# Another order of the parts of an attention step, and one more copy of the transposed keys on VectorE

## The chip, the cores and the metric

The kernel runs on one core of a Trainium2 chip. Its time is device microseconds (us) of one execution. Engines are named as the profile names them: PE is TensorE's matmul, PEld its weight loads, DVE is VectorE, ACT is ScalarE, POOL is GpSimd, SP is SyncE, which issues the DMAs. Each engine works through its own queue in order.

## The reference

Three parts follow each other; everything is float32.

```python
# attention, q, k, v: (4, 8, 576, 64)
out_d = sm_attn(q_d, k_d, v_d)          # on means of 4 tokens
out_up = np.repeat(out_d, factor, axis=2)
mask = np.abs(pos[:, None] - pos[None, :]) < factor
...
out_local = np.matmul(attn, v)          # softmax over the band of 7 tokens
x = out_up + out_local                  # -> (2304, 512)
# soft mixture of experts, 8 experts with 4 slots each
logits = x @ phi
slot_input = softmax(logits, axis=0).T @ x
h = np.maximum(slot_input[e] @ w1[e], 0.0); slot_out[e] = h @ w2[e]
y = softmax(logits, axis=1) @ slot_out
# feed-forward
h = np.maximum(y @ w_in, 0.0)
out = h * h @ w_out
```

## The kernel before

The attention works on 16 units; a unit is one batch and a pair of heads, four units make a batch. It is a software pipeline written out by hand: step s of 19 runs a string of letters, each letter is one part, and the part is that of unit s minus the letter's lag (table LAG). All steps use the string ORDER, except those in the table ORDERS (0 to 3 and 15 to 18 before). The order of the letters is the order of the instructions in each engine's queue; two parts that use different engines don't see each other's place in the string.

The parts that matter here, with their engines:

- Q, L (SP): load q and k, or v, of a unit; l and o (SP): load the next LOADN or LOADO expert weights into a ring of 32 buffers.
- T, K (PE, then ACT and DVE): transpose q, or k, of a unit into two PSUM tiles `tr`, one for each head (line 412), and copy each by two copies, of 64x320 and 64x256, into `qt` (line 423) or `kz` (line 419). The tuple DCOPY names the (is k, head, half) whose copy DVE makes; ACT makes the others. One `qt` and one `kz` buffer serve all units.
- M, S (PE): the band mask and the local scores into the bank `s` (lines 443, 454). R (DVE): their maximum and its subtraction (465, 466); E (ACT): exp (471); n (DVE): sums and reciprocal (501, 502); P (POOL): probabilities `pl` (508); p (PE, DVE): their transposes and copies `pt` (527, 528).
- d, b (POOL): sums of four tokens of q and of k (436, 438). s (PE): scores of those (479); m (DVE): maxima (486, 487); e (ACT): exps `pd` (493); N (DVE, POOL): normalisation `sm` and `pn` (515 to 517); q (PE, ACT, DVE): transposes `pdp` and copies `pdt` (556, 557).
- V, v, w, D, A: values (570), their sums and transposes (537, 545, 547), the downsampled values and their scaled copy `xd` on ACT (583, 588), and the addition `xt` on DVE (596).
- t, X, Y: logits of a unit (612), token rows (631, 639). With the last unit of a batch, t also issues the batch softmax `mb`, `nm`, `ee`, `eb` on DVE and ACT (655 to 668), and g and G its transposes and the sum `sip` and `acc` (676 to 700).
- F, H, J (PE): so many filler matmuls of 128x256 in bf16 (line 364), whose result nobody reads; table FN gives the number for each step. START is the number of fillers ahead of step 0. c: a step of narrowing the feed-forward weights, if they are there (CONV).

Below, "S of unit 9" is the part S, and "the letter q" the part q. After step 18 comes a chain that closes the batch softmax (lines 812 to 838, ending with `sT`), then eight experts (888 to 917), then the feed-forward (1044 to 1138).

Of the kernel before, what the change touches and what calls it, by code (L numbers as in the profile page):

```python
# [18 lines left out]
B, H, S, D = 4, 8, 576, 64  # L19
# [16 lines left out]

MAG_LO = 2.0 ** -15
MAG_HI = 1.875 * 2.0 ** 16 - 2.0 ** -7
CONV = {10: 1, 12: 1, 15: 3, 18: 1, 19: 2}
TCH = 384  # L40
LOOK = 2
W32 = 5
LBE = 5
LOADN = {0: 1, 1: 2, 2: 2, 3: 2, 4: 1, 5: 3, 6: 4, 7: 3, 8: 3, 9: 2, 10: 2, 11: 4, 12: 3, 13: 4, 14: 4, 15: 2, 16: 4, 17: 3, 18: 4, 19: 4}
LOADO = {0: 1, 1: 1, 2: 1, 3: 0, 4: 2, 5: 0, 6: 1, 7: 0, 8: 0, 9: 0, 10: 2, 11: 0, 12: 2, 13: 0, 14: 0, 15: 3, 16: 1, 17: 4, 18: 3, 19: 4}
ORDER = 'YFSgREVLvqwndGKHJsmDPeTAoptQMbNXcl'
LAG = {'Q': -2, 'L': 0, 'T': 0, 'K': 0, 'd': 1, 'b': 0, 'M': 0, 'S': 1, 'R': 1, 's': 1, 'E': 1, 'm': 1, 'n': 1, 'P': 1, 'e': 1, 'N': 1, 'v': 2, 'q': 2, 'p': 1, 'w': 2, 'V': 2, 'D': 2, 'A': 2, 't': 2, 'X': 2, 'Y': 3, 'g': 3, 'G': 3}
LASTS = 3
ORDERS = {0: 'YAsFvSgKToGdpDlHqJRPcEVewnMNXtQbmL', 1: 'YSgREVFvqdJwnGKLsmDAPeToHlptQbMcNX', 2: 'YFcVSgRLEvqJwnKdsmPDAeToptQbHlGMNX', 3: 'YgSREVLFvqJwnKdsmDAeToHPGplctQbMNX', 15: 'YJSgREVFLvqwndKsmDAeToPHGpctQbMlNX', 16: 'YFSgREVLvqJdwnKlsmGDAeToPHpctQbMNX', 17: 'YJEFSgRVLvqwnPTKdsMDAmeoGHlctQbNXp', 18: 'YEVFLvqJSgDeRwnKdsmAToGHPlptQbcMNX'}
FN = {'F': [0, 1, 1, 0, 0, 0, 0, 0, 0, 0, 0, 0, 0, 0, 0, 4, 0, 10, 0, 0], 'H': [10, 5, 2, 0, 0, 0, 0, 0, 0, 0, 0, 0, 0, 0, 0, 1, 0, 4, 0, 0], 'J': [1, 4, 3, 0, 0, 0, 0, 0, 0, 0, 0, 0, 0, 0, 0, 0, 7, 3, 0, 0]}  # L50
LATE = 16
LOADS = 'Q0 L0 phi Q1 L1'
START = 24
DDVE = ()
DCOPY = ((1, 0, 1),)
PCOPY = (0, 5, 4)
CHAIN = (2, 4, 4)
NEG = -6.25e7
# [23 lines left out]
def attention_moe_ffn_kernel(  # L82
# [105 lines left out]
    def load_next(n=1):  # L188
        for _ in range(n):
            if not loads or not free:  # L190
                return
            kind, i, j = loads[0]

            fits = [x for x in free if x[0] is not wa or kind in ("w1", "w2") and i == 0 and int(x[1][1:]) >= WRES]
            fits.sort(key=lambda x: x[0] is not wa)
            if kind == "wout" or kind == "win" and (j > 0 or LPOS[i] > 50 or lb is None) or kind != "win" and i == NE - 1:
                fits = [x for x in free if x[0] is ring]
            elif kind != "win" and i >= LBE + 1:
                fits = [x for x in fits if x[1][0] != "b"]
                fits.sort(key=lambda x: x[0] is ring)  # L200

            if kind == "wout" or kind == "win" and j > 0:
                if sum(x[0] is ring for x in free) <= 2 + parts[0]:
                    return
            if not fits:
                return
            place = fits[0]
            free.remove(place)
            loads.popleft()
            load(kind, i, j, place)  # L210
# [87 lines left out]
    def narrow_next(n=1):  # L298
        for _ in range(n):
            narrow_turn()  # L300
# [10 lines left out]
    with tc.tile_pool(name="att", bufs=1, side="right") as ap:  # L311
# [49 lines left out]
        def busy(n, start=False):  # L361

            for _ in range(n):
                nc.tensor.matmul(warm, warmb, warmw, start=start, stop=True, skip_group_check=True)  # L364
# [38 lines left out]
        def transposes(u, js=(0, 1)):  # L403
            st = U[u]
            for j in js:
# [7 lines left out]
                for h, t in enumerate(ts):  # L413
                    hr = slice(64 * h, 64 * h + 64)
                    to = (kzs[u % QKB][hr, h] if j else qs[u % QKB][hr])[:, 3:3 + S].rearrange("p (c r) -> p c r", r=9)
                    for r in range(2):
                        o, i_ = to[:, :, r:9:2], t[64 * r:64 * r + 64, 0:5 - r].rearrange("p i c -> p c i")
                        if j:
                            (nc.vector.tensor_copy if (j, h, r) in DCOPY else nc.scalar.copy)(out=o, in_=i_)  # L419
                        elif (j, h, r) in DCOPY:  # L420
                            nc.vector.tensor_scalar(out=o, in0=i_, scalar1=1.0 / 128.0, scalar2=None, op0=ALU.mult)
# [346 lines left out]
        def run(x, s):  # L768
# [6 lines left out]
            elif x in "lo":  # L775
                load_next((LOADN if x == "l" else LOADO).get(s, 1))
            elif x in FN:
                busy(FN[x][s])
            elif x == "c":
                narrow_next(CONV.get(s, 0))  # L780

# [5 lines left out]
        tm.enter_context(tc.manual_schedule())  # L787
        busy(START, True)
        for s in range(NU + LASTS):
            for x in ORDERS.get(s, ORDER) + ("a" if s == LATE else ""):  # L790
                if x == "a":
# [405 lines left out]
```

## Time and profile before

| | us |
|---|---|
| median of 3 runs | 432.02 (431.2 to 434.45) |
| the profiled execution | 431.98 |
| its span, first to last instruction | 430.3 |
| mean granted TensorE clock in the span | 0.992 |

Between the profiled execution and its span lie 1.7 us outside all instructions. The attention fills the first 153 us, the closing chain ends with `sT` at 161.7 us, the experts run to 197 us and the feed-forward to the end. A row of the timeline gives start, duration, engine, line and operation; several instructions of one kind are merged with their count, and their duration is then from the first start to the last end. In brackets stands the idle time of the engine before the row, with what released it.

### The profile page before, as it was taken

What the parts mean: (1) busy time and instruction counts of PE and PEld (TensorE: products, weight loads), DVE (VectorE), ACT (ScalarE), POOL (GpSimd) and SP (SyncE); (2) the same over time, 40 slices, a digit from 0 to 9 for tenths busy, and PEclk for the clock granted to TensorE, in tenths of its full rate; (3) what the DMA queues carried; (4) which work ended last, traced back from release to release, by engine and by line L of the source; (5) the groups of instructions that cost most, each with busy time, mean ns of one, the idle gap of its engine ahead of it and who ended that gap; (6) DMA issues with size and microseconds to landing.
All of it is one profiled execution on the core that took longest, in us unless ns stands there. A gap on an engine that the chain in (4) does not pass through costs nothing.

```text
span 430.3 us, 11647 instructions
## 1 busy us (share of the span) xinstructions
PE 402.4 (94%) x4534; PEld 308.2 (72%) x4534; DVE 300.7 (70%) x713; ACT 270.6 (63%) x670; POOL 116.2 (27%) x225
## 2 busy tenths in 40 slices
PE   7798899899998989997999999999999999999994
PEld 5566667657766755554877888888888888888883
DVE  3566666666666542396999897897899777665663
ACT  4578768767867422245897587777875655545640
POOL 7576556655656300130000600005000320000000
PEclk9999999999999989999999999999999999999998
DMA  6998999999831489999990001020000000012232
GB/s 178 366 254 259 291 293 340 274 282 288 208 96 33 149 249 368 411 407 407 408 390 8 0 0 50 1 100 0 2 0 0 2 1 2 0 74 75 75 133 87
DMA packets 43249, 70.55 MB, mean 164 GB/s; under 512 B 24378, under 2 KB 24634, under 8 KB 43194
## 3 DMA queue, kind: packets, MB, share of 16 engines
q1 hardware_dynamic: 43050, 69.68, 49.1%
q8 instruction: 36, 0.59, 0.6%
q14 instruction: 19, 0.16, 0.1%
q10 hardware_dynamic: 144, 0.13, 0.1%
HBM read 65.07 MB, written 4.72 MB: 162 GB/s over the span
## 4 chain that ended last, share of the span: by engine, by line
PE 59%; DVE 3%; ACT 1%; issue 1%; DVEq 0%; ACTq 0%
PE po L1125 44%; PE up L1044 4%; PE so L917 4%; PE hp L888 3%; PE ap L1002 1%; DVE glo L1057 0%; DVE part L1107 0%; PE lgt L364 0%; DVE r L1053 0%; PE warm L930 0%; PE ctp L722 0%; DVE win L234 0%; DVE win L233 0%; PE arp L1015 0%; PE crp L867 0%
## 5 line engine op out<-in xcount | busy, mean ns | idle before, releaser
L1125 PE MATMUL po<-wparts,ghi 128*128 128x512 f32 x576 | 148.8, 392 | 0.2 <-DVE part L1107 0.2
L1125 PEld LDWEIGHTS po<-wparts,ghi 128*128 128x128 f32 x576 | 106.8, 188 | 20.5 <-DVE part L1107 0.6
L1125 PE MATMUL po<-wparts,glo 128*128 128x512 f32 x288 | 81.7, 391 | 0.5 <-DVE glo L1057 0.5
L1049 ACT ACTIVATE r<-up 128x384 f32<-128x384 f32 x96 | 47.0, 490 | 55.5 <-PE up L1044 48.2
L1057 DVE TENSOR_TENSOR glo<-r,ghi 128x384 fp32r<-128x384 f32 x94 | 52.2, 558 | 22.0 <-ACT ghi L1056 18.6
L1125 PEld LDWEIGHTS po<-wparts,glo 128*128 128x128 f32 x288 | 54.0, 188 | 13.3 <-DVE glo L1057 0.9
L1029 POOL COPY selq<-asb 32x128 f32<-32x128 f32 x48 | 20.3, 422 | 138.0 <-ACT asb L1010 135.4
L1053 DVE TENSOR_TENSOR r<-r 128x384 f32<-128x384 f32 x48 | 26.8, 559 | 17.4 <-ACT ghi L1052 17.4
L1044 PE MATMUL up<-cst,ast 128*128 128x384 f32 x96 | 33.0, 344 | 1.1 <-ACT cst L874 1.1
L508 POOL TENSOR_TENSOR pl<-elp,sm 64x350 f32<-64x350 f32 x32 | 24.6, 770 | 31.9 <-PE tr L412 21.9
L419 ACT COPY kz<-tr 64x320 f32<-64x320 f32 (+1 forms) x48 | 20.5, 428 | 15.1 <-PE tr L412 14.3
L423 ACT ACTIVATE qt<-tr 64x320 f32<-64x320 f32 x64 | 28.0, 437 | 1.2
L1052 ACT ACTIVATE ghi<-r 128x384 fp32r<-128x384 f32 x50 | 26.3, 526 | 1.6
L1055 ACT ACTIVATE r<-r 128x384 f32<-128x384 f32 x46 | 24.2, 526 | 1.5
L465 DVE TENSOR_REDUCE mx<-s 128x10 f32<-128x350 f32 x16 | 8.3, 517 | 23.3 <-PE s L454 23.3
L1056 ACT CAST ghi<-r 128x384 fp32r<-128x384 f32 x46 | 23.6, 514 | 1.4
L436 POOL TENSOR_TENSOR s<-kz 64x288 f32<-64x288 f32 x32 | 21.2, 661 | 5.9 <-DVE kz L419 3.8
L1109 DVE TENSOR_TENSOR part<-po,part 128x512 f32<-128x512 f32 x36 | 22.6, 683 | 0.0
L1044 PEld LDWEIGHTS up<-cst,ast 128*128 128x128 f32 x96 | 18.0, 188 | 5.9 <-ACT cst L874 1.6
L471 ACT ACTIVATE elp<-elp 128x350 f32<-128x350 f32 x16 | 7.9, 496 | 20.8 <-DVE elp L466 20.8
L454 PE MATMUL s<-kz,qt 128*29 128x70 f32 x640 | 13.0, 225 | 7.5 <-ACT qt L423 7.5
L517 POOL TENSOR_TENSOR pn<-pd,sm 128x435 f32<-128x435 f32 x16 | 14.6, 914 | 15.5 <-DVE sm L516 7.9
(209 smaller groups left out, 715.0 us busy)
## 6 DMA issues: line engine op xcount, KB each, us to landing
w<-in_moe_w_dram SPq DMA_DIRECT2D x64, 512.0 KB, 7.6
win<-in_moe_w_in_dram SPq DMA_DIRECT2D x16, 512.0 KB, 10.2
wout<-in_moe_w_out_dram SPq DMA_DIRECT2D x16, 512.0 KB, 10.2
vw<-in_v_dram SPq DMA_DIRECT2D x62, 80.0 KB, 6.0
q<-in_q_dram SPq DMA_DIRECT2D x16, 288.0 KB, 5.7
k<-in_k_dram SPq DMA_DIRECT2D x16, 288.0 KB, 5.9
out_dram<-o SPq DMA_DIRECT2D x17, 256.0 KB, 2.1
vw<-in_v_dram SPq DMA_DIRECT2D x2, 64.0 KB, 2.7
```

What stands on the lines that cost most here:

```text
L423: nc.scalar.mul(out=o, in_=i_, mul=1.0 / 128.0)
L436: nc.gpsimd.tensor_tensor(out=s1[r], in0=t[:, :, 0], in1=t[:, :, 1], op=ALU.add)
L508: nc.gpsimd.tensor_tensor(out=pl[r, :, c0:c0 + W], in0=el[r], in1=sm[r, 0:NB].unsqueeze(2).to_broadcast([64, NB, W]), op=ALU.mult,)
L1044: nc.tensor.matmul(t, ast[:, 128 * f:128 * f + 128], cst[:, c * n:c * n + n], start=True, stop=True)
L1049: nc.scalar.activation(out=r, in_=t, func=AF.Relu)
L1052: nc.scalar.activation(out=ghi, in_=r, func=AF.Square)
L1053: nc.vector.tensor_tensor(out=g, in0=r, in1=r, op=ALU.mult)
L1055: nc.scalar.activation(out=g, in_=r, func=AF.Square)
L1056: nc.scalar.copy(out=ghi, in_=g)
L1057: nc.vector.tensor_tensor(out=glo, in0=g, in1=ghi, op=ALU.subtract)
L1109: nc.vector.tensor_tensor(out=part[c, i], in0=po[c][i], in1=part[c, i], op=ALU.add)
L1125: nc.tensor.matmul(po[c][i], a[:, 128 * i:128 * i + 128], w[f], start=(first and w is whi and a is ghi), stop=(last and a is glo), skip_gr ...
```

## The change

It changes tables only. DCOPY gets a second entry: the 64x320 copy of the first head's transposed k, made by ACT before, is made by DVE in every unit. (These are transposed keys of the attention; the copies of slot probabilities further down are as they were.) ORDER and ORDERS put the letters in another order; step 3 now uses ORDER. START falls from 24 to 12 and FN gives the fillers to other steps. LOADN, LOADO and CONV are changed at some steps.

```diff
-CONV = {10: 1, 12: 1, 15: 3, 18: 1, 19: 2}
+CONV = {5: 1, 7: 1, 10: 2, 11: 1, 14: 1, 15: 2, 19: 3}
...
-ORDER = 'YFSgREVLvqwndGKHJsmDPeTAoptQMbNXcl'
+ORDER = 'clYSRgVdEvqHJwFnLGKsmoDAeTPpbNQtXM'
...
-FN = {'F': [0, 1, 1, 0, 0, 0, 0, 0, 0, 0, 0, 0, 0, 0, 0, 4, 0, 10, 0, 0], 'H': [10, 5, 2, 0, 0, 0, 0, 0, 0, 0, 0, 0, 0, 0, 0, 1, 0, 4, 0, 0], 'J': [1, 4, 3, 0, 0, 0, 0, 0, 0, 0, 0, 0, 0, 0, 0, 0, 7, 3, 0, 0]}
+FN = {'F': [0, 1, 5, 0, 0, 0, 0, 0, 0, 0, 0, 0, 0, 0, 0, 3, 0, 9, 0, 0], 'H': [8, 6, 1, 0, 0, 0, 0, 0, 0, 0, 0, 0, 0, 0, 0, 3, 6, 7, 1, 0], 'J': [2, 7, 5, 0, 0, 0, 0, 0, 0, 0, 0, 0, 0, 0, 0, 0, 5, 2, 0, 0]}
...
-START = 24
+START = 12
 DDVE = ()
-DCOPY = ((1, 0, 1),)
+DCOPY = ((1, 0, 1), (1, 0, 0))
```

Seen by engine: POOL's queue is the same, row for row. ACT's loses the 16 copies of 64x320 and is otherwise the same from the second step on. DVE's gains them, no narrowing moves to another place in it, and the two small operations of N stand in another place in three steps. On PE, M and X change places in the steps, and the fillers are elsewhere (83 before the chain, 80 in the old kernel). On SP the same loads stand in another order among each other.

**DVE, the step that ends the second batch** (`sm` is N's, `mb` to `lst` the batch softmax, `acc` the letter G's, `kz` the letter K's, `mx<-sdb` the letter m's). Before:

```order
L528 COPY pt<-sdb 128x2x58
L655 TENSOR_REDUCE mb_1799<-lgt 128x1
...
L645 COPY lst<-lgt 128x16
L515 TENSOR_SCALAR sm_1671<-sm_1671 128x3
L516 RECIPROCAL sm_1671<-sm_1671 128x3
L465 TENSOR_REDUCE mx_1863<-s_1817 128x10
...
L698 SCALAR_TENSOR_TENSOR acc<-acc,al_1801,sip_1918 128x512
```

Now:

```order
L528 COPY pt<-sdb 128x2x58
L515 TENSOR_SCALAR sm_1675<-sm_1675 128x3
L516 RECIPROCAL sm_1675<-sm_1675 128x3
L655 TENSOR_REDUCE mb_1818<-lgt 128x1
...
L645 COPY lst<-lgt 128x16
L465 TENSOR_REDUCE mx_1866<-s_1838 128x10
...
L698 SCALAR_TENSOR_TENSOR acc<-acc,al_1820,sip_1926 128x512
L419 COPY kz_146<-tr_10_1933 64x64x5
L419 COPY kz_146<-tr_10_1933 64x64x4
L486 TENSOR_REDUCE mx_1866<-sdb 128x2
```

N's two operations moved ahead of the batch softmax; the copy of 64x64x5 is new, between `acc` and the old copy. In the steps that end no batch, that copy is the only difference.

**PE, the first units** (`tr_1*` is k's transpose, `tr_0*` q's; 175 and 177 are unit 0's, 187 unit 1's k). Before:

```order
L364 MATMUL lgt<-warmb 128x256
L412 MATMUL tr_10_219<-ident,k_177 128x64
...
L412 MATMUL tr_01_236<-ident,q_175 64x64
L364 LDWEIGHTS warmb
...
L454 MATMUL s_266<-kz_146,qt_143 29x70
...
L412 MATMUL tr_11_312<-ident,k_187 64x64
L479 MATMUL sdb<-qkd 64x144 x2
```

Now:

```order
L412 MATMUL tr_01_208<-ident,q_175 64x64
L364 LDWEIGHTS warmb
...
L412 MATMUL tr_10_231<-ident,k_177 128x64
...
L454 MATMUL s_261<-kz_146,qt_143 29x70
...
L412 MATMUL tr_11_293<-ident,k_187 64x64
L364 LDWEIGHTS warmb
...
L479 MATMUL sdb<-qkd 64x144 x2
```

Before, 24 fillers, k, q, 11 fillers, M, S of unit 0, 5 fillers, k of unit 1 and directly the letter s. Now 12 fillers, q, 8 fillers, k, 2 fillers, M, 1 filler, S, k of unit 1, then 13 fillers ahead of the letter s. In the next step 5 fillers stand between w and k of unit 2, where 3 stood ahead of w.

**PE, the last units** (`av<-pdt,vd` is D of unit 14, `ptp` and `sdb<-ident,pl` the letter p of unit 15, the last, `av<-pt,vw` its V). Before:

```order
L583 MATMUL av_0_2932<-pdt_2957,vd_2981 64x48 x4
L527 MATMUL ptp_0_3010<-ident,pl 128x128 x4
L527 MATMUL sdb<-ident,pl 128x128
...
L639 MATMUL av_1_2933<-ident,xt_3002 64x128
L364 LDWEIGHTS warmb
...
L570 MATMUL av_0_3058<-pt,vw_140 64x73
```

Now:

```order
L583 MATMUL av_0_2929<-pdt_2954,vd_2968 64x48 x4
L364 LDWEIGHTS warmb
...
L527 MATMUL ptp_0_3011<-ident,pl 128x128 x4
L527 MATMUL sdb<-ident,pl 128x128
...
L639 MATMUL av_1_2930<-ident,xt_2999 64x128
L364 LDWEIGHTS warmb
...
L570 MATMUL av_0_3055<-pt,vw_140 64x73
```

Six fillers stand ahead of p, where none stood; ahead of V it is 9 fillers, 13 before. Between D of unit 15 and the letter t of that unit it is 9, 4 before.

## Rows read from the trace of the kernel before

**Rows 1.** The page's head: span, and busy time of each engine.

```profile
span 430.3 us, 11647 instructions
PE 402.4 (94%) x4534; PEld 308.2 (72%) x4534; DVE 300.7 (70%) x713; ACT 270.6 (63%) x670; POOL 116.2 (27%) x225
```

**Rows 2.** Timeline of PE in a regular step: start, duration, operation, [idle before].

```profile
96.76 0.82 PE L454 MATMUL s<-kz,qt 128*29 128x70 f32 x40 [0.52 <-ACT qt L423]
...
99.50 0.67 PE L412 MATMUL tr<-ident,k 64*128 64x64 f32 x10
...
100.73 0.77 PE L583 MATMUL av<-pdt,vd 75*64 75x96 f32 x16
...
104.85 0.37 PE L454 MATMUL s<-kz,qt 128*29 128x70 f32 x10 [0.53 <-ACT qt L423]
```

**Rows 3.** Timeline of ACT in the same step.

```profile
100.21 1.34 ACT L419 COPY kz<-tr 64x320 f32<-64x320 f32 x3 [0.18 <-PE tr L412]
101.60 0.41 ACT L588 ACTIVATE xd<-av 128x288 f32<-128x288 f32 x1
101.91 0.37 ACT L493 ACTIVATE pd<-sdb,mx 128x144 f32<-128x144 f32 x1
...
102.97 1.82 ACT L423 ACTIVATE qt<-tr 64x320 f32<-64x320 f32 x4
```

**Rows 4.** Timeline of DVE in the same step.

```profile
100.69 0.43 DVE L419 COPY kz<-tr 64x256 f32<-64x256 f32 x1 [0.56 <-ACT kz L419]
```

**Rows 5.** Waits of 0 to 140 us: engine and line, releaser, total, times, longest.

```profile
PEld av L583 <- ACT kz L419: 2.0, 10, 0.2
```

**Rows 6.** Groups of 0 to 140 us by form: busy us, mean ns of one, idle before.

```profile
L528 DVE COPY pt<-ptp 128x464 f32<-128x464 f32 x15 | 9.5, 634 | 1.3 <-PE ptp L527 1.3
...
L419 DVE COPY kz<-tr 64x256 f32<-64x256 f32 x16 | 6.9, 431 | 9.2 <-ACT kz L419 8.9
```

**Rows 7.** Timeline of the step that ends the second batch.

```profile
87.24 1.21 PE L570 MATMUL av<-pt,vw 64*64 64x73 f32 x40
...
87.55 0.92 POOL L517 TENSOR_TENSOR pn<-pd,sm 128x435 f32<-128x435 f32 x1 [2.50 <-ACT xr L640]
...
91.82 0.75 DVE L698 SCALAR_TENSOR_TENSOR acc<-acc,al,sip 128x512 f32<-128x512 f32 x1 [1.61 <-PE sip L695]
...
92.64 0.43 DVE L419 COPY kz<-tr 64x256 f32<-64x256 f32 x1
```

**Rows 8.** Timeline of the first units.

```profile
1.15 5.30 PE L364 MATMUL lgt<-warmb 128*128 128x256 bf16 x24 [1.15 <-DVE warmb L315]
...
12.30 0.34 PE L479 MATMUL sdb<-qkd 64*64 64x144 f32 x2
...
14.25 0.46 DVE L486 TENSOR_REDUCE mx<-sdb 128x2 f32<-128x288 f32 x1
...
17.76 0.82 PE L454 MATMUL s<-kz,qt 128*29 128x70 f32 x40
...
20.80 0.52 PE L412 MATMUL tr<-ident,k 64*128 64x64 f32 x10 [0.22 <-ACT pdt L557]
```

**Rows 9.** The load of unit 1's k: issue, and us from issue to landing.

```profile
L376 SPq DMA_DIRECT2D k<-in_k_dram x1: 430/430/430, 6.0 to 6.0; - x1
...
DMA to landing us min/median/max: 4.2/4.2/4.2
```

**Rows 10.** Timeline of PE in the last two steps.

```profile
147.33 1.58 PE L364 MATMUL lgt<-warmb 128*128 128x256 bf16 x13
...
151.95 0.61 PE L364 MATMUL lgt<-warmb 128*128 128x256 bf16 x4
...
153.44 0.54 PE L612 MATMUL lgt<-xt,phis 128*32 128x128 f32 x16 [0.88 <-DVE xt L596]
```

**Rows 11.** Stretches around 154 us: length, busy of each engine, PEclk, DMA share, GB/s.

```profile
152.00:153.50 1.50, 0.62 (x10) 0.32 (x12) 0.83 (x2) 0.41 (x1) 0.00 (x0) 1.00 0.91 232
...
154.50:155.50 1.00, 1.00 (x7) 0.64 (x6) 0.37 (x4) 0.70 (x3) 0.00 (x0) 0.50 1.03 332
```

More of the change, by code (lines that the diff above doesn't have):

```diff
@@ L43 @@
 LBE = 5
-LOADN = {0: 1, 1: 2, 2: 2, 3: 2, 4: 1, 5: 3, 6: 4, 7: 3, 8: 3, 9: 2, 10: 2, 11: 4, 12: 3, 13: 4, 14: 4, 15: 2, 16: 4, 17: 3, 18: 4, 19: 4}
-LOADO = {0: 1, 1: 1, 2: 1, 3: 0, 4: 2, 5: 0, 6: 1, 7: 0, 8: 0, 9: 0, 10: 2, 11: 0, 12: 2, 13: 0, 14: 0, 15: 3, 16: 1, 17: 4, 18: 3, 19: 4}
-ORDER = 'YFSgREVLvqwndGKHJsmDPeTAoptQMbNXcl'
+LOADN = {0: 1, 1: 2, 2: 2, 3: 3, 4: 2, 5: 2, 6: 4, 7: 3, 8: 3, 9: 2, 10: 2, 11: 4, 12: 3, 13: 3, 14: 4, 15: 2, 16: 4, 17: 2, 18: 4, 19: 4}
+LOADO = {0: 1, 1: 1, 2: 1, 3: 0, 4: 3, 5: 0, 6: 1, 7: 0, 8: 0, 9: 2, 10: 2, 11: 0, 12: 1, 13: 0, 14: 0, 15: 3, 16: 2, 17: 4, 18: 3, 19: 4}
+ORDER = 'clYSRgVdEvqHJwFnLGKsmoDAeTPpbNQtXM'
 LAG = {'Q': -2, 'L': 0, 'T': 0, 'K': 0, 'd': 1, 'b': 0, 'M': 0, 'S': 1, 'R': 1, 's': 1, 'E': 1, 'm': 1, 'n': 1, 'P': 1, 'e': 1, 'N': 1, 'v': 2, 'q': 2, 'p': 1, 'w': 2, 'V': 2, 'D': 2, 'A': 2, 't': 2, 'X': 2, 'Y': 3, 'g': 3, 'G': 3}
 LASTS = 3
-ORDERS = {0: 'YAsFvSgKToGdpDlHqJRPcEVewnMNXtQbmL', 1: 'YSgREVFvqdJwnGKLsmDAPeToHlptQbMcNX', 2: 'YFcVSgRLEvqJwnKdsmPDAeToptQbHlGMNX', 3: 'YgSREVLFvqJwnKdsmDAeToHPGplctQbMNX', 15: 'YJSgREVFLvqwndKsmDAeToPHGpctQbMlNX', 16: 'YFSgREVLvqJdwnKlsmGDAeToPHpctQbMNX', 17: 'YJEFSgRVLvqwnPTKdsMDAmeoGHlctQbNXp', 18: 'YEVFLvqJSgDeRwnKdsmAToGHPlptQbcMNX'}
-FN = {'F': [0, 1, 1, 0, 0, 0, 0, 0, 0, 0, 0, 0, 0, 0, 0, 4, 0, 10, 0, 0], 'H': [10, 5, 2, 0, 0, 0, 0, 0, 0, 0, 0, 0, 0, 0, 0, 1, 0, 4, 0, 0], 'J': [1, 4, 3, 0, 0, 0, 0, 0, 0, 0, 0, 0, 0, 0, 0, 0, 7, 3, 0, 0]}
+ORDERS = {0: 'SRYFAGTgHKesqEVvPcnLJwdDlNQbpmoXMt', 1: 'YwFgSREVdcvqKnLHlJsmPeATGbpXMoNQDt', 2: 'YFSRgEVvqdwnLJKlsmPDcAeTGpbtoXMNQH', 15: 'YFcSRgEVHvqwdlnLJGKsmPDeATbpNQtoXM', 16: 'YFSRgEVGvqwdclnLKJsPmDATeHpbtoXMNQ', 17: 'gTYFGEVcvqKwDlnLeJAbHmtpoPsdNQSRXM', 18: 'YFcvSRgVEeHqwdJlnLGsDmPTAbpNQtoKXM'}
+FN = {'F': [0, 1, 5, 0, 0, 0, 0, 0, 0, 0, 0, 0, 0, 0, 0, 3, 0, 9, 0, 0], 'H': [8, 6, 1, 0, 0, 0, 0, 0, 0, 0, 0, 0, 0, 0, 0, 3, 6, 7, 1, 0], 'J': [2, 7, 5, 0, 0, 0, 0, 0, 0, 0, 0, 0, 0, 0, 0, 0, 5, 2, 0, 0]}
 LATE = 16
 LOADS = 'Q0 L0 phi Q1 L1'
-START = 24
+START = 12
 DDVE = ()
-DCOPY = ((1, 0, 1),)
+DCOPY = ((1, 0, 1), (1, 0, 0))
 PCOPY = (0, 5, 4)
```

## The prediction, made before the run

> **What bounds the kernel now.** I read the page's head first, then the timeline of one step, engine by engine, and last the two ends of the attention, where the order changes most. PE is busy 402 of 430 us [rows 1], so time can only come out of stretches in which PE waits or does work that nobody needs. The change touches the attention, the first 153 us; what follows gets the same queues, only sooner or later.
>
> In a regular step the reader should see a relay between two engines. PE runs without a gap from S at 96.76 to the end of D at 101.50 (100.73 + 0.77) [rows 2]. ACT starts `xd` at 101.60, when D has ended, then the exps at 101.91, then the q copies from 102.97 for 1.82 us to 104.79 [rows 3], and the next S starts at 104.85, having kept PE idle for 0.53 us [rows 2]. So a step of 8.09 us (104.85 - 96.76) is 4.74 us of PE and 3.35 us of ACT behind it.
>
> **The change, part by part.** The sum is made against the profiled execution, 431.98 us, which lies 0.04 us under the median of the three runs.
>
> *The copy of the keys, regular steps.* ACT makes three copies from 100.21 to 101.55 [rows 3]. One goes, a third of 1.34, so 0.45 us, and ACT would be free at 101.1. But `xd` waits for D, which ends at 101.50: ACT's gain is hidden behind PE. On DVE the old copy starts at 100.69, because it waited 0.56 us for ACT's copy of the same tile, and ends at 101.12 [rows 4]. Now DVE makes the pair itself, from about 100.21. The new copy has 320 elements. The nearest rows are 431 ns for 256 elements and 634 ns for 464 [rows 6]; along the line between them it is 0.49 us, with these two as bounds. The pair then ends at 101.13 (100.21 + 0.49 + 0.43), as before. The maxima and the exps behind it stay where they are: 0 us. With the upper bound the pair ends 0.15 us later, over 13 regular steps 2 us more; with the lower one nothing is gained, since `xd` still waits for D. The lower bound of this term is a different one: the row that names ACT's key copy as what D's weights waited for, 10 times 0.2 us [rows 5]. Were it a true wait, up to 2.0 us could go. I take 0: D follows s, and the 0.2 us is only the time for which a loaded weight waits for PE.
>
> *N ahead of the batch softmax, three steps.* `pn` starts late, at 87.55, after 2.50 us idle, and ends at 88.47 [rows 7]. Now it is early. But q must also wait for V, which ends at 88.45 [rows 7]: the gain is 0.02, with the weight loads at best 0.14 us. Against it, in these steps `acc` holds DVE until 92.57 and the old copy follows at 92.64, ending at 93.07 [rows 7]. ACT had made the first copy beside `acc`; now the pair comes after it and ends at 93.49 or so (92.57 + 0.92), 0.25 us later when 0.17 is taken off for the overlap of one DVE operation with the next and a G that starts earlier. Net +0.1 us per step, +0.3 in all; between -0.4 (three times the best gain) and +1.3 (three times 0.42).
>
> *M behind X; loads; narrowing.* X and M run while PE waits for the q copies, with 0.53 us to spare [rows 2]: 0 us; if that cover were gone, each would cost its own length in either order. DVE's queue shows no narrowing step at another place, so CONV does nothing. The loads are the same ones, issued some steps sooner or later, on SP behind the same waits; no row of PE, ACT or DVE in the attention names a DMA. 0 us; if the load of a q came late, K of that unit would wait for it and the step would grow by as much.
>
> *The start.* Before, 24 fillers hold PE from 1.15 for 5.30 us [rows 8]. Now q, then k, are transposed earlier and S of unit 0 comes earlier too, but k of unit 1 lands only at 10.2 (6.0 + 4.2) [rows 9], as before. Its transposes, 0.52 us [rows 8], end at 10.8. Then come 13 fillers, 1.58 us as the 13 later ones took [rows 10], to 12.3; so s starts where it did, at 12.30 [rows 8]. It takes 0.56 us (from 99.50 + 0.67 to 100.73) [rows 2] to 12.9. But the maxima, which before started at 14.25, behind K's copies [rows 8], now have these behind them and start at 13.0: 1.2 us sooner, and with them the exps, the q copies and S of unit 1, 17.76 before. In the next step the 5 fillers between w and K cost 0.61 us (5 x 0.12). Before, K of unit 2 came 3.04 us after S (20.80 - 17.76) [rows 8]; now it comes 2.74 us as in a regular step (99.50 - 96.76) [rows 2] plus 0.61, so 0.31 us worse. I count 0.45 between 0.31 and 0.61. Net -0.75 us, from -0.9 to -0.6.
>
> *The end.* Nine fillers ahead of the last V instead of 13, at 0.12 each [rows 10]: -0.49, of which p, pushed by six fillers (0.73 us) into what was mostly a wait, gives some back. I take -0.3, between -0.49 and 0.24 (all six pushed through). Behind the last D, PE works 0.61 us and then idles 0.88 us before t [rows 10], so five more fillers, 0.6 us, are covered. Without that cover they would cost 0.6.
>
> PE was busy only 0.62 of the 1.5 us before 153.5, and from about 154 the granted clock is 0.50, the lower level, 1.2 GHz [rows 11]. PE's transposes in the closing chain then run at half speed. With more fillers just before, I expect the higher level to hold. The chain alternates between PE and the others; over the three microseconds at the lower level about 1.3 us of the chain are PE's, which halve: -0.65. Bounds: 0 (the clock falls all the same) and -1.5 (all of the stretch is PE's).
>
> Sum: 0 + 0.3 - 0.75 - 0.3 - 0.65 = -1.4, so **430.6 us**.
>
> **A rule against it.** At the very start 24 fillers take 0.22 us each [rows 8] and later ones 0.12 [rows 10]: the first ones run at the lower level. The Trainium skill (TensorE: Matmul & The Clock Gate, "What's actually happening") holds that the throttled state is the default and that PE's activity releases it. By that rule halving START works against the change, and the first rival below, 432.3 us, is the result. The trace agrees in the two filler durations above.
>
> **The rivals.**
>
> 1. *The clock falls at the start: slower.* Between S of unit 0 and the landing of unit 1's k, PE now has nothing for over a microsecond, and only a few fillers before. That is like the stretch before 153.5, after which the level fell [rows 11]. The 13 fillers would then take 0.22 us each, 1.3 us more, and K and s about 0.4 more, all on the path to S of unit 1: 430.6 + 1.7 = 432.3. It decides if PE's clock is at 0.50 when these fillers run. For it: the idle wait. Against: 20 fillers of 0.22 us, 4.4 us, and both transposes stand ahead of that wait.
> 2. *The clock falls at the end all the same.* Nine fillers don't hold it: 430.6 + 0.65 = 431.3, and with rival 1 too 433.
> 3. *The step itself gets shorter.* [Rows 5] is a true wait and ACT's 0.45 us come into the relay: 0.2 us in 13 steps, 428.0; with all of 0.45 in each, 424.8. Against it: `xd` starts 0.10 us after D in [rows 2, 3].
> 4. *DVE is last.* The new copy takes 0.63 us: +2 us in regular steps, +0.4 at the ends of batches: 433.
> 5. *Nothing moves the path*: fillers and copies are hidden before and after: 432.0.
>
> **How the numbers follow.** The forecast gets 0.40, rival 1 0.24, rival 2 0.13, rival 3 0.11, rival 4 0.06, rival 5 0.06. The likeliest time is 430.6. The range runs from 428.4, which leaves out the stronger part of rival 3 and an unseen gain, to 433.2, which takes in rivals 1, 2, 4 and 5. About 1% (4.3 us) is what a measurement of this kernel can tell from no change. Only the strong form of rival 3 and something that no row shows go beyond it on the fast side: 0.07. Beyond it on the slow side lies only a sum of rivals 1, 2 and 4 or a load that comes late: 0.04. Within 1%: 0.89.
>
> **What would show it.** In the profile after: ACT's key copies two per step and `xd` still 0.1 us behind D, steps of 8.09 us (right) or under 7.9 (rival 3); maxima behind a pair of DVE copies of about 0.9 us, or over 1.05 (rival 4); S of unit 1 near 16.5, or past 18 with a clock of 0.50 at 10 to 14 us (rival 1); no stretch at 0.50 near 153 us, or one (rival 2); `sT` near 160.3 instead of 161.7. It is wrong if a regular step changes by more than 0.1 us, or if PE waits for a DMA.

## The result and the profile after

The changed kernel took 434.77 us in the median of 20 executions (430.38 to 437.33), the kernel before 431.22 on the same chip. The ratio is 1.0052, with a 95% interval from 1.0028 to 1.0075: slower by half a per cent, where 430.6 us and a little faster had been forecast. The ratio leaves out three of the 20 executions, which were over 1.5% slower than the fastest one; by the medians of all it is 1.0082. The profiled execution took 435.10 us:

```profile
span 433.4 us, 11666 instructions
PE 404.0 (93%) x4537; PEld 308.5 (71%) x4537; DVE 310.2 (72%) x729; ACT 264.0 (61%) x654; POOL 116.0 (27%) x225
```

Beside [rows 1], ACT is busy 6.6 us less and DVE 9.5 us more, and the span is 3.1 us longer. Where these come from is read from the start of S in each unit:

| start of | before | after | difference |
|---|---|---|---|
| S of unit 1 | 17.76 | 15.72 | -2.04 |
| S of unit 5 | 51.02 | 48.55 | -2.47 |
| S of unit 7 | 69.60 | 67.43 | -2.17 |
| S of unit 8 | 77.69 | 80.08 | +2.39 |
| S of unit 11 | 104.85 | 107.85 | +3.00 |
| S of unit 12 | 112.93 | 117.19 | +4.26 |
| S of unit 15 | 140.11 | 145.01 | +4.90 |
| t of unit 15 | 153.44 | 157.92 | +4.48 |
| sT | 161.43 | 165.35 | +3.92 |
| end of the span | 430.3 | 433.4 | +3.1 |

So the start and the end gained in this execution, as forecast, and the middle lost 7.4 us: 4.6 in the step of unit 7 (12.65 us), 1.3 in that of unit 11 (9.34 instead of 8.08 us) and 1.6 in the three steps that end a batch (units 5, 9 and 13). The waits of PE from 0 to 145 us, as [rows 5] (total, times, longest):

```profile
PE s L454 <- ACT qt L423: 5.8, 13, 0.7
PE tr L412 <- DMA k<-in_k_dram: 4.3, 3, 2.6
...
PE av L570 <- issue: 0.9, 1, 0.9
...
PE av L570 <- DMA vw<-in_v_dram: 0.8, 3, 0.4
```

In the kernel before no line of this list names a DMA. The longest of these three waits, 2.6 us, is in the step of unit 7, for the k of unit 8. In the step of unit 11 PE waits for no load: there V stands still for 0.92 us until 110.00, the row "issue", which means that PE waited for nothing that the profile shows (the last section comes back to it). The step of unit 7 on PE, by its timeline:

```profile
67.43 0.81 PE L454 MATMUL s<-kz,qt 128*29 128x70 f32 x40 [0.47 <-ACT qt L423]
...
69.15 0.68 PE L570 MATMUL av<-pt,vw 64*64 64x73 f32 x4 [0.37 <-DMA vw<-in_v_dram]
...
74.42 0.52 PE L412 MATMUL tr<-ident,k 64*128 64x64 f32 x10 [2.61 <-DMA k<-in_k_dram]
...
76.20 0.71 PE L412 MATMUL tr<-ident,q 64*128 64x64 f32 x10
76.84 1.11 PE L527 MATMUL ptp<-ident,pl 128*128 128x128 f32 x4
...
80.08 0.33 PE L454 MATMUL s<-kz,qt 128*29 128x70 f32 x8
```

V waits for its v piece by piece, K waits 2.61 us for the k of unit 8, and behind that wait the transposes take longer than in a regular step (0.71 for 0.52, 1.11 for 0.66 us). From 70 to 80 us the granted clock is 0.83 in the mean. The same stretch in SP's timeline:

```profile
65.44 0.33 SPq L376 DMA_DIRECT2D k<-in_k_dram  x1
...
DMA to landing us min/median/max: 8.6/8.6/8.6
```

The last line is from the list of this load alone. The same load in the kernel before:

```profile
59.06 0.42 SPq L376 DMA_DIRECT2D k<-in_k_dram  x1
```

Now the k is issued 9.0 us ahead of its K, and for 2.61 of these K waits: it could have started 6.4 us behind the issue, and the k lands 8.6 us behind it. In the kernel before K followed the issue by 13.3 us (59.06 to 72.34), and the k took 4.3 us to land. By the order of SP's queue 23 weight tiles now stand ahead of it instead of 17. SP's own waits for the landing of weight tiles grew with that, from 9.7 to 30.4 us in four lines of its list up to 140 us, of which these are two of the changed kernel:

```profile
SPq L182 <- DMA w<-in_moe_w_dram: 9.7, 7, 2.0
SPq L376 <- DMA w<-in_moe_w_dram: 7.6, 9, 1.5
```

A step without such a wait (unit 10) answers to [rows 2 to 4], on PE, ACT and DVE:

```profile
99.76 0.81 PE L454 MATMUL s<-kz,qt 128*29 128x70 f32 x40 [0.46 <-ACT qt L423]
...
103.73 0.77 PE L583 MATMUL av<-pdt,vd 75*64 75x96 f32 x16
...
107.85 0.37 PE L454 MATMUL s<-kz,qt 128*29 128x70 f32 x9 [0.47 <-ACT qt L423]
```

```profile
103.26 0.88 ACT L419 COPY kz<-tr 64x320 f32<-64x320 f32 x2 [0.23 <-PE tr L412]
104.60 0.41 ACT L588 ACTIVATE xd<-av 128x288 f32<-128x288 f32 x1 [0.46 <-ACT kz L419]
```

```profile
103.22 0.93 DVE L419 COPY kz<-tr 64x320 f32<-64x320 f32 x2
104.19 0.46 DVE L486 TENSOR_REDUCE mx<-sdb 128x2 f32<-128x288 f32 x1
```

The relay is what it was: D ends at 104.50, `xd` starts at 104.60, and the step takes 8.09 us. ACT's copies end 0.46 us ahead of `xd`, which gains nothing from it.

At the end of the attention PE's timeline, as [rows 10], and two stretches, as [rows 11]:

```profile
152.26 1.15 PE L364 MATMUL lgt<-warmb 128*128 128x256 bf16 x9
...
156.44 1.16 PE L364 MATMUL lgt<-warmb 128*128 128x256 bf16 x9
157.92 0.47 PE L612 MATMUL lgt<-xt,phis 128*32 128x128 f32 x16 [0.33 <-DVE xt L596]
```

```profile
156.50:158.00 1.50, 1.17 (x14) 0.81 (x17) 0.83 (x2) 0.41 (x1) 0.00 (x0) 1.00 0.76 240
159.00:160.00 1.00, 0.58 (x4) 0.43 (x5) 0.38 (x3) 0.73 (x3) 0.00 (x0) 1.00 1.09 401
```

Ahead of t PE is now busy 1.17 of 1.5 us, for 0.62, and the clock stays at 1.00 behind it. From S of unit 15 to t it takes 12.91 us (13.33 before), from t to `sT` 7.43 (7.99).

### The profile page after: what moved, and what is told of

It is laid out like the page before. It is cut to its first block, busy times and chain, and to the rows that moved or that the text cites. A ratio compares the mean times of both kernels' runs of the same rounds, so it can differ in the third digit from the quotient of the medians.

```text
span 433.4 us, 11666 instructions
## 1 busy us (share of the span) xinstructions
PE 404.0 (93%) x4537; PEld 308.5 (71%) x4537; DVE 310.2 (72%) x729; ACT 264.0 (61%) x654; POOL 116.0 (27%) x225
## 4 chain that ended last, share of the span: by engine, by line
PE 58%; DMA 2%; DVE 2%; ACT 1%; issue 1%; DVEq 0%; ACTq 0%
PE po L1125 45%; PE up L1044 4%; PE hp L888 3%; PE so L917 2%; DMA wout<-in_moe_w_out_dram 2%; PE ap L1002 1%; PE lgt L364 0%; PE ctp L722 0%; DVE win L233 0%; DVE win L234 0%; PE arp L1015 0%; DVE glo L1057 0%; PE stp L836 0%; PE sip L695 0%; PE sip L689 0%
## 5 line engine op out<-in xcount | busy, mean ns | idle before, releaser
L419 ACT COPY kz<-tr 64x320 f32<-64x320 f32 (+1 forms) x32 | 13.6, 424 | 13.3 <-PE tr L412 12.8
L419 DVE COPY kz<-tr 64x320 f32<-64x320 f32 (+1 forms) x32 | 14.6, 457 | 5.8 <-PE tr L412 5.0
```

## The experiments

Two things had to be told apart: the loads, and the new places of the work on the engines. A run to run spread of several microseconds lies over all ratios, so each is read beside the steps of its trace.

**1. The loads of before in the changed kernel.**

```
-LOADN = {..., 3: 3, 4: 2, 5: 2, ...}   LOADO = {..., 4: 3, ..., 9: 2, ...}
+LOADN = {..., 3: 2, 4: 1, 5: 3, ...}   LOADO = {..., 4: 2, ..., 9: 0, ...}
-ORDER = 'clYSRgVdEvqHJwFnLGKsmoDAeTPpbNQtXM'
+ORDER = 'cYSRgVdEvqHJwFnLGKsmDAeTPpbNoQtXMl'
```

> The changed kernel with the weights queued as before (the two tables of weight loads and the places of their letters): from unit 5 on, each k then has as many weight tiles ahead of it on SP as in the kernel before (17 ahead of the k of unit 8, against 23 in the change). Theory A, the loads: the waits of PE for k and for v (4.3 and 0.8 us in the change) go, the step of unit 7 falls from 12.65 to about 8.1 us and that of unit 11 from 9.34 to 8.1, so S of unit 15 starts near 139.2 instead of 145.0; the experts and the feed-forward behind gave 0.8 us back in the change and give nothing back now, so the time falls by 5 us, to about 430 on the scale on which the kernel before is 431.2. Rival B, the order itself: the long steps come from the new order on PE and DVE, the late k only coincides; then the time stays within 1 us of the change, at 434 to 435.

Measured: ratio 0.9975 (0.9941 to 1.0009), 0.0077 or 3.3 us under the change; by the two intervals taken together, 1.6 to 5.1 us. That rules out rival B, and 5 us is at the edge. No wait of PE in this profile behind the start names a DMA, and the steps of units 7 and 11 are back at 8.38 and 8.10 us. S of unit 15 starts at 141.13, not at 139.2, because the start took 1.9 us more in this execution (experiment 3). The loads are the larger part of the loss. (The tiles ahead of each k are as in the kernel before from unit 6 on; ahead of the k of units 2, 3 and 5 they are one or two fewer.)

**2. The loads of the change in the kernel before.**

```
-ORDER = 'YFSgREVLvqwndGKHJsmDPeTAoptQMbNXcl'
+ORDER = 'lYFSgREVLvqwndGKHJsmoDAPeT...'   (l first, o behind m, in all orders)
+LOADN, LOADO of the change
```

> The kernel before with only the weights queued as in the change. Theory A: PE waits for k in the steps of units 5 to 11; S of unit 7 starts at 69.6 here against 67.43 in the change, so 2.2 us less is waited in that step, some 2.4 us, and about 1 us in that of unit 11: slower than before by 2 to 4 us, about 434. Rival B: the loads alone do nothing, 431.2 within 0.5 us.

Measured: ratio 1.0105 (1.0048 to 1.0161), 4.5 us slower, by six executions. The size is that of theory A, the mechanism is not quite: in this execution no K waits. PE stands still in the middle of the D in the step of unit 6 and works at the lower level afterwards, as PE's timeline and then the stretches show (length, busy time of PE, PEld, DVE, ACT and POOL, granted clock, DMA share, GB/s):

```profile
64.65 0.76 PE L583 MATMUL av<-pdt,vd 75*64 75x96 f32 x15
67.84 0.34 PE L583 MATMUL av<-pdt,vd 75*64 75x48 f32 x1 [2.42 <-issue]
```

```profile
66.00:68.00 2.00, 0.16 (x1) 0.17 (x1) 0.00 (x0) 0.00 (x0) 1.65 (x3) 0.87 1.06 341
68.00:70.00 2.00, 2.00 (x16) 1.50 (x16) 0.84 (x3) 1.74 (x8) 0.00 (x0) 0.50 1.03 394
70.00:72.00 2.00, 2.00 (x23) 1.62 (x22) 1.07 (x4) 1.39 (x4) 0.75 (x1) 0.50 1.01 370
```

"issue" is a wait for nothing that the profile shows. It costs 2.4 us itself and about 2 more through the clock, which is at 0.50, 1.2 GHz, from 68 us on: the steps of units 6 and 7 take 11.56 and 8.99 us instead of twice 8.09. The last section comes back to it. So the loads cost time in either order; that all of it comes through late k is not shown.

**3. N behind t again, and the copy on ACT again**, each on top of experiment 1:

```
-ORDER = 'cYSRgVdEvqHJwFnLGKsmDAeTPpbNoQtXMl'
+ORDER = 'cYSRgVdEvqHJwFnLGKsmDAeTPpboQtNXMl'
```

> e1 with N (the normaliser of the downsampled part: two DVE operations and the multiplication on POOL) behind t again in a regular order, as before. It matters in the three steps that end a batch. Theory A2: with N ahead, the multiplication on POOL runs beside the batch softmax, whose maximum of two tensors on DVE then takes 0.84 instead of 0.16 us, the transposes of the weights start late, and V behind them on PE starts 1.7 to 1.8 us after S instead of 1.1. With N back, V starts at 1.1 again and the maximum takes 0.16: against e1 less 0.5 to 0.7 us in the steps of units 9 and 13 and under 0.2 us in that of unit 5 (which has no such maximum), 1.2 us in all. Rival: V's delay is hidden behind what waits for the maxima of the scores, so the steps keep their 10.8 to 11.3 us and the time is that of e1.

```
-DCOPY = ((1, 0, 1), (1, 0, 0))
+DCOPY = ((1, 0, 1),)
```

> e1 with the copy of the first head's keys on ACT again, as before. In a regular step nothing changes (the activation xd waits for D): 0 us. In the three steps that end a batch the pair of copies on DVE stands behind acc and the maxima behind the pair start 0.7 us later in the change; without it the exps start 0.15 us sooner: 0.45 us less than e1 in all. Rival: the third copy on ACT is late itself in these steps and xd with it, so nothing is gained, 0 us; or the copy on DVE helped in regular steps and its loss costs up to 0.1 us in each of 13, 1.3 us more than e1.

Measured: ratios 0.9961 (0.9930 to 0.9992) and 0.9956 (0.9930 to 0.9982). The steps that end a batch (units 5, 9, 13) took 10.46, 11.23, 11.33 us in experiment 1; with N back 10.61, 10.82, 10.83, which is 0.76 us less; with the copy back 10.32, 11.06, 11.15, which is 0.49 us less. Both go the expected way. N ahead gains 0.15 us in unit 5 and costs 0.41 and 0.50 where a batch has a predecessor. The place is seen in the changed kernel's DVE, POOL and PE around 88 us, where [rows 7] had `pn` at 87.55 and V 1.12 us behind S:

```profile
87.54 0.18 DVE L516 RECIPROCAL sm<-sm 128x3 f32<-128x3 f32 x1
87.63 0.28 DVE L655 TENSOR_REDUCE mb<-lgt 128x1 f32<-128x144 f32 x1
87.95 0.84 DVE L657 TENSOR_TENSOR mb<-mb,mb 128x1 f32<-128x1 f32 x1
```

```profile
87.86 0.91 POOL L517 TENSOR_TENSOR pn<-pd,sm 128x435 f32<-128x435 f32 x1 [0.38 <-DVE sm L516]
```

```profile
90.27 1.16 PE L570 MATMUL av<-pt,vw 64*64 64x73 f32 x40
```

The same operation in the kernel before (minimum, median and longest in ns):

```profile
L657 DVE TENSOR_TENSOR mb<-mb,mb x3: 159/159/161, 85.2 to 154.4; 128x1 f32<-128x1 f32 x3
```

A maximum of 128x1 takes 0.84 us, against 0.16 in the kernel before, and ends when POOL's `pn` does. The exponential on ACT, the two transposes of the weights on PE and V, which stands behind these, are late by it: V starts 1.70 us after S (88.57).

The fillers and the first loads were the same in six profiled kernels (the change, experiment 1, both of this one, experiment 4 and the first of 5). S of unit 1 came at 15.72 and 16.41 in two of them and at 17.65 to 18.16 in four. PE in the run with N back, beside [rows 8], and its stretches:

```profile
7.22 0.81 PE L454 MATMUL s<-kz,qt 128*29 128x70 f32 x40 [0.68 <-ACT kz L419]
10.39 0.60 PE L412 MATMUL tr<-ident,k 64*128 64x64 f32 x10 [2.36 <-DMA k<-in_k_dram]
10.92 2.96 PE L364 MATMUL lgt<-warmb 128*128 128x256 bf16 x13
13.81 0.47 PE L479 MATMUL sdb<-qkd 64*64 64x144 f32 x2
```

```profile
8.00:10.00 2.00, 0.03 (x4) 0.00 (x0) 1.04 (x2) 0.49 (x1) 1.77 (x4) 1.00 0.95 266
10.00:11.00 1.00, 0.61 (x11) 0.48 (x12) 0.00 (x0) 0.00 (x0) 0.91 (x2) 0.85 1.06 140
11.00:14.00 3.00, 3.00 (x17) 1.92 (x21) 1.56 (x4) 0.83 (x2) 1.14 (x2) 0.50 0.95 341
```

PE idles 2.36 us for the k of unit 1, the clock falls, and 13 fillers take 2.96 us. In the changed kernel's own profile this wait was 1.38 us, the clock stayed at 1.00, and the same fillers took 1.59 us:

```profile
9.58 0.52 PE L412 MATMUL tr<-ident,k 64*128 64x64 f32 x10 [1.38 <-DMA k<-in_k_dram]
10.04 1.59 PE L364 MATMUL lgt<-warmb 128*128 128x256 bf16 x13
```

S of unit 1 comes 2.39 us later in the run with N back than in the change; 0.81 of that is the later K, and most of the rest the 1.37 us that the fillers take more.

**4. The batch maximum with one tensor less** (on top of experiment 1, N ahead):

```
-nc.vector.tensor_tensor(out=mb, in0=mb, in1=G[b - 1]["mb"], op=ALU.max)
+nc.vector.tensor_scalar(out=mb, in0=mb, scalar1=G[b - 1]["mb"], scalar2=None, op0=ALU.max)
```

> The changed kernel with the loads as before and N ahead (as in the first run), in which the maximum with the earlier batch's maximum (128x1, two tensors) is written as an operation on one tensor with a scalar per partition: the same numbers, one tensor read less. Theory: what holds this operation for 0.84 instead of 0.16 us is POOL's multiplication beside it, through the reads of two tensors; as one tensor and a scalar it takes 0.16 us, V starts 1.1 to 1.3 us after S in the steps of units 9 and 13 instead of 1.7 and 1.8, and these steps fall from 11.23 and 11.33 to about 10.85. Rival: it is held by the queue or by what it waits for, whatever its operands: 0.84 us again.

```profile
L657 DVE TENSOR_SCALAR mb<-mb,mb x3: 212/214/214, 86.1 to 154.6; 128x1 f32<-128x1 f32 x3
```

Minimum, median and longest: 0.21 us, though `pn` runs on POOL from 86.00 to 86.92 here as well. The steps of units 9 and 13 fall to 10.69 and 10.73. So it was the pair of tensors beside `pn`, not the queue. The Trainium skill (SBUF — State Buffer, "Who interferes with whom") says just this: a DVE operation with two inputs in SBUF contends with a GpSimd operation that reads SBUF, one with a single input does not, outside the modes in which DVE takes the shared port as well. The trace agrees in the 844, 159 and 214 ns.

**5. The three parts undone together, and two other starts on top of that**: the 13 fillers ahead of K; q and k of unit 1 issued first.

```
+ORDER = 'cYSRgVdEvqHJwFnLGKsmDAeTPpboQtNXMl'   DCOPY = ((1, 0, 1),)
```

> The changed kernel with three parts undone together: the weights queued as before, N behind t, the copy of the first head's keys on ACT. What is left of the change are its start, its end, X ahead of M and the other places. Theory: the three parts cost what the runs so far gave for each (loads 0.0077 of the time, N 0.76 us and the copy 0.49 us in the steps that end a batch), and start and end keep their gains: steps of 8.1 us, 10.5 at the ends of batches, ratio to the kernel before near 0.9945 (1.0052 - 0.0077 - 0.0018 - 0.0011), 429 us on the scale on which before is 431.2. Rival: what is left gains nothing since the clock falls at the start (wait for k of unit 1) in most executions: ratio 0.998 to 1.000.

```
-1: 'YwFgSREVdcvqKnLHJsmPeATGbpXMoNQDtl'
+1: 'YwFgSREJHVdcvqKnLsmPeATGbpXMoNQDtl'
```

> The same, with the 13 fillers of the first steps moved from behind the transposes of unit 1's keys to ahead of them, into the time in which PE waits for that k (1.4 to 2.4 us in four profiles; the granted clock was at 0.50 for 2.5 to 3.5 us behind this wait in two of them). Theory: the clock stays at 1.00, and s follows K directly instead of 1.6 us later: S of unit 1 at 15.0 to 15.6 instead of 15.7 to 18.1, about 1.3 us less than the kernel with three parts undone, in the mean. Rival: s then waits for POOL or the copies instead, S of unit 1 stays at 15.7 or later and only the fall of the clock is avoided; or the fillers are late themselves and nothing changes.

```
-LOADS = 'Q0 L0 phi Q1 L1'
+LOADS = 'Q0 Q1 L0 phi L1'
```

> The kernel with three parts undone, with q and k of unit 1 issued before v of unit 0 and phi. Theory: k of unit 1 is issued near 2 us instead of 6.0 and lands by 8 us, so PE doesn't wait for it, K of unit 1 follows S of unit 0 at 8.2 us instead of 9.6 to 10.4, and S of unit 1 starts near 14.5; 1.5 to 2.5 us less than the kernel with three parts undone. Rival: the DMA engines are the limit in the first 8 us, q and k of unit 1 hold up those of unit 0, S of unit 0 starts 1 us later or more and the gain is lost; or v of unit 0 comes late for V at 16 us.

Measured: 0.9990 (0.9956 to 1.0024), 0.9958 (0.9924 to 0.9992) and 0.9971 (0.9938 to 1.0005). The first is the rival's number, not the 0.9945 added up from parts, and it lies above experiment 3, of which it should have been the sum: intervals of 0.003 each way don't carry sums of such parts. Its steps are as expected (10.48, 10.61, 10.62 at the ends of batches), its S of unit 1 at 18.16. In the other two PE doesn't wait for k, but s waits for POOL until 11.02 in both, so S of unit 1 comes at 16.24 and 15.63, not at 15.0 and 14.5. With all 13 fillers spent ahead of K, the next idle stretch (12.2 to 14.0, ahead of p) was followed in the first of them by a clock of 0.50 and 0.52 from 15 to 18 us.

**6. The end alone**: the kernel before with one number changed, 9 fillers for 4 behind the last D.

```
-'H': [10, 5, 2, 0, ..., 1, 0, 4, 0, 0]
+'H': [10, 5, 2, 0, ..., 1, 0, 9, 0, 0]
```

> The kernel before with one number changed: 9 fillers instead of 4 behind the last D. Theory: PE's clock does not fall near 153.7, the stretch at 0.50 up to 157 goes, t starts when it did after the last S (13.33 us behind) and the time from t to sT falls from 7.99 to 7.43 us as in the change. Rival: the five fillers don't hold the clock, or it was held in the change by the fillers further ahead (9 for 13 before the last V, X in another place): 7.99 us again and a stretch at 0.50.

```profile
151.06 1.16 PE L364 MATMUL lgt<-warmb 128*128 128x256 bf16 x9
152.54 0.47 PE L612 MATMUL lgt<-xt,phis 128*32 128x128 f32 x16 [0.33 <-DVE xt L596]
```

```profile
154.00:155.00 1.00, 0.72 (x12) 0.41 (x11) 0.61 (x3) 0.83 (x3) 0.00 (x0) 1.00 0.95 332
```

t starts 13.32 us after the last S, as before, and no stretch is at 0.50; from t to `sT` it takes 7.31 us instead of 7.99. The idle time ahead of t is 0.33 us here and was 0.88 [rows 10]: the five fillers cost nothing. That they hold the clock, this one execution doesn't show, for in experiment 2 the old four fillers and the same idle time were followed by no fall either:

```profile
156.90 0.47 PE L612 MATMUL lgt<-xt,phis 128*32 128x128 f32 x16 [0.88 <-DVE xt L596]
...
158.00:159.00 1.00, 0.61 (x5) 0.45 (x5) 0.40 (x3) 0.75 (x3) 0.00 (x0) 1.00 0.84 299
```

There, too, it takes 7.31 us from t to `sT`. With four fillers the clock fell in one profile of two, with nine in none of twelve (7.31 to 7.48 us).

**7. Putting it together, and fewer loads at a time.** From experiment 1: the copy on ACT, N ahead with the one-tensor maximum, q and k of unit 1 first, 7 fillers between K and s and 10 ahead of p. Then the same with the 36 tiles spread evenly, and with the tiles held back (of the 50 entries of the first row only 36 load a tile, since the buffers are full by then):

```
 loads in steps 0 to 14 (both tables together)
 first:   2 3 3 2 3 3 5 3 3 2 4 4 5 4 4
 spread:  2 3 2 2 3 2 3 2 2 3 2 3 2 2 3
 late:    1 1 1 1 1 1 1 1 1 4 4 4 4 4 4
```

> What the runs so far point to, put together: the changed kernel with the weights queued as before, the copy on ACT, N ahead but the batch maximum as one tensor and a scalar, q and k of unit 1 issued first, and the fillers of the first steps laid into PE's waits (7 between K and s, 10 between the q transposes and p). Theory: S of unit 1 starts at 15.6 with the clock at 1.00, the steps at the ends of batches take 10.3 to 10.6 us, the end is that of the change: in a run without waits for instructions S of unit 15 starts at 137.5 to 138 and the first expert product at 158 to 158.5, 3.5 us before the kernel before; ratio 0.990 to 0.994. Rival: waits of PE for nothing that the profile shows, with a fall of the clock behind them, fall into the steps of units 3 to 10 whatever the order, and the ratio stays at 0.996 to 0.998 as in the other runs.

> The same with the 36 weight tiles spread evenly over the steps, two or three in each until step 14, instead of up to five, 4 to 6 fewer of them ahead of the k of units 9 to 13. Theory: the DMA engines are less full in steps 4 to 10, the unexplained waits of PE there grow rarer and with them the falls of the clock: 1 us less than the run with the same start, mean granted clock 0.998 or more in most executions. Rival: the waits do not depend on the queue and the two times are the same; or tiles that come later are missed by the experts and the time is longer by up to 2 us.

> The run before the last with the weight tiles held back: one tile in each of steps 0 to 8, four in each of steps 9 to 14, so that DMA carries about 1.4 MB in a step of 8.1 us up to unit 8 (some 175 GB/s, by the bytes of the loads) and 2.9 MB later. Theory: the waits of PE that the profile puts down to nothing (0.3 to 1.7 us, in eleven of thirteen profiles so far, the most of them in the steps of units 3 to 8) come from full DMA queues; with little in them none stands in units 1 to 7, the clock does not fall there, and the mean granted clock of an execution is 0.998 or more in most of them (4 of 12 with the tiles spread evenly); S of unit 9 starts near 82.5 us. Behind it the loads are dense: if a wait comes, it comes in the steps of units 9 to 14. Rival: the waits come as before at the same places of the program, whatever DMA does, and the time is that of the kernel with the tiles spread, or up to 4 us more where the experts wait for tiles that come late.

Measured: 0.9931 (0.9886 to 0.9975), 0.9929 (0.9892 to 0.9966) and 0.9919 (0.9882 to 0.9957): by these ratios all three beat both kernels, the last by 3.5 us over the kernel before (428.46 us in the median). By the medians of all executions the ratios are 0.9998, 0.9907 and 0.9926, so the gain of the first hangs on which executions are counted. The three can't be told apart.

Executions with a mean granted clock of 0.998 or more were 3 of 12 and 4 of 12 for the first two and 9 of 12 with the tiles held back; 3 of 20 for the change, none of 6 in experiment 2, and 3 to 6 of 12 in experiments 1, 3 and 5. For the kernel before they were 37 of 97, but from 5 of 23 beside the first two to 17 of 29 beside experiment 1, and 6 of 17 beside the last. So the light queue has the largest share, and counts that differ as much for one kernel don't prove by themselves that the queue made it. The last one's page:

```profile
span 425.5 us, 11659 instructions
...
PEclk9999999999999999999999999999999999999999
DMA  6866556799999989999990001020000000022123
```

In the attention no wait of its PE names "issue" or a DMA, and S of unit 9 starts at 82.89. The dense loads from 80 us on brought the experts no loss: `sT` comes at 158.01.

## Why the prediction was wrong, step by step

The step that failed is "M behind X; loads; narrowing", in its sentence that the loads are the same ones, issued sooner or later: "0 us". The price was named there (K waits if a load comes late) and not weighed, and the prediction's own sign of being wrong came: PE waits for a DMA. What it missed was in reach: the number of weight tiles ahead of each k in SP's queue (23 for 17 at unit 8), and a DMA share of 0.96 or more in five of the six stretches of 10 us from 10 to 70 us of the kernel before. That no PE row of before names a DMA shows only that there was slack, not how much. For the k of unit 8 the lead from issue to K was 13.3 us and the landing took 4.3 (up to 8.4 for another k), so the slack was 9 us, or 5 by the slowest landing. The change took 6.9 us of the lead (13.3 to 6.4), and in its fuller queue this k took 8.6 us to land. By times the term is +3.3 us (experiment 1), not 0. How much of these 3.3 us is waiting for k is open: in the profiles with these loads time goes to late k and v (unit 7) and to waits for "issue" (unit 11, and experiment 2).

- **The copy, regular steps: right.** 8.09 us, `xd` 0.10 behind D, a pair of 0.93 us for an estimated 0.92.
- **The copy at the ends of batches: nearly right**, 0.49 us in three steps, 0.16 in each, where 0.25 had been put in.
- **N ahead: wrong in sign, by a term that was left out.** A gain of 0.02 to 0.14 in each step was forecast; it cost 0.76 us in all. With the copy the steps that end a batch lost 1.25 us, at the upper bound (1.3) of a term put at 0.3. The step "q must also wait for V" held, but V itself was taken as fixed. It waits on PE behind the transposes of the batch softmax, and that softmax ran beside POOL's multiplication. The gain itself was there: with the maximum on one tensor (experiment 4) the three steps are 0.12, 0.13 and 0.10 us shorter than with N back.
- **The start: the mechanism right, the result mostly rival 1.** Where the clock held, S of unit 1 came 2.04 and 1.35 us sooner, for the 1.2 forecast. Where it fell, nothing was gained. Over six profiles the mean is 17.35, against 17.40 over three with the old start (17.76, 17.38, 17.05): about 0 for -1.2. The next step lost 0.20 us in the change (8.45 for 8.25), where 0.45 had been put in. Rival 1 named the condition and had a chance of 0.24; four of six would have been nearer.
- **The end: right from S to t, in part luck behind it.** 0.42 us for 0.3 from S to t, and the same in ten of the eleven profiles with the new end (13.42 us instead of 12.91 with the tiles held back). From t to `sT` it is 0.56 for 0.65 in the two profiles compared, but the old order takes 7.31 us as well when its clock holds (experiment 2), less than the 7.43 of the change. So the gain is there only in executions in which the old end loses the clock; how many these are is not known.
- Rivals 2, 3 and 4 did not come: no stretch at 0.50 around t (157.92) in the change, no shorter step, a copy within its estimate.

The range ended at 433.2 because a late load was priced at nothing. Put together afterwards, the terms as measured are 3.3 for the loads, 1.25 for the ends of batches, 0.2 for the start (no gain up to S of unit 1, then 0.20) and up to -1.0 for the end, 3.8 us or more; the ratio gives 2.2 (1.2 to 3.2) on the prediction's scale and the two profiles 3.1. Terms read from single executions add up no better than that.

## What to carry to other kernels

When a change moves transfers in a queue, count what stands ahead of each load that an engine waits for, and set its lead (issue to use) against its landing time; slack that no wait shows can still be used up. A wait of PE costs about twice its length when its clock falls behind it (2.4 and about 2 us in experiment 2), so fillers belong inside the wait, and the first place to put prefetches is where the DMA engines have room. Before moving a POOL operation, look which DVE operations on two tensors it will then run beside.

## What the runs showed that was not expected

A DVE maximum of 128 numbers took 0.84 us beside a POOL multiplication and 0.21 us once it read one tensor.

The waits of PE for "issue", 0.17 to 2.42 us long, stood in eleven of the first thirteen profiles, 17 in all and all of them before 111 us, and in five kernels at the D in the step of unit 3. The Trainium skill (Runtime: NRT & Kernel Launch, "Instruction fetch mechanics") says that an engine's instructions come by DMA in blocks of 16 KiB, 256 instructions, and that this fetch is mostly hidden. The traces agree on the blocks, but here the fetch is not always hidden. The changed kernel's page has 36 packets of that size in all:

```profile
q8 instruction: 36, 0.59, 0.6%
```

Each trace lists start and end of every packet, and all instructions of PE in order (matmuls, weight loads and the sequencer's own). Counted through, all 17 waits stand at one place of a block: ahead of the waiting instruction are 193 more than a multiple of 256 (1217 at the D of unit 3). The packet that belongs to the block in order had ended 1.37 to 1.81 us before each wait ended, and in none of the fourteen profiles did any block start less than 1.28 us behind its packet. So these waits are for late instruction blocks. With the tiles held back the packets up to 85 us ended 2.7 to 6.4 us ahead of their blocks, in the kernel before 1.4 to 4.6. Under the dense loads behind 85 us one block, at 116.81, again started 1.41 us behind its packet, after 0.82 us of idle PE that the profile puts down to DVE, and that step took 8.42 us instead of 8.10. That a full queue makes the packets late fits all of this; of the light queue there is one profile.
